# Four stores of a late output piece as operations of their own, and a new order of the last products

## The chip, the core and the metric

The kernel runs on one core of one Trainium2 chip. Times are device microseconds (us) of that core. The profile and its trace come from one profiled execution; "span" is the time from its first to its last recorded instruction. TensorE is called PE, VectorE DVE, ScalarE ACT, GpSimd POOL and SyncE SP, as the profile calls them.

## What is computed

An attention block with polynomial sketch features is followed by a token-mixing block. The attention output of all 4 heads is x, of shape 4 batches x 1088 tokens x 128. Then (reference, cut):

```python
theta = x @ w_theta
zr, zi = x * cos(theta), x * sin(theta)
y = einsum('ts,bsd->btd', w_tok_r, zr) + einsum('ts,bsd->btd', w_tok_i, zi)
u = x + y
out = u + maximum(u @ w_ch, 0)
```

The sum over 1088 source tokens in y is most of the matrix work. `out` is 4 x 1088 x 128 in float32.

## The kernel before

The program is a list of some thousand operations, each with an engine, the buffers that it reads and writes, and a Python function that issues its instructions. Two tables written out by hand decide everything that a scheduler would: `ORDER` is the order in which the operations are issued (each engine works through its own in that order), and `SLOTS` gives each buffer the slot of its class (`big`: 22 slots, one row of token weights each; `g1`, `g3`: output tiles; `ps`: the eight PSUM banks). Waits follow from both: an instruction waits for the producers of its data, and for the last users of its slot.

Batches 0 and 1 go through `mix_row`. Batches 2 and 3 (`PAIR`) are mixed together by `winograd`: seven products of half-size blocks instead of eight, named "1" to "7". Each has 8 or 9 matmuls (one for each 128 source tokens) for each of two column pieces of a half of 544 tokens (`PARTS`: 384 and 160). A finished product is added on DVE to the half that it belongs to, and `done` calls `finish` for both pieces. The text below names the last pieces so:

- **Q384** and **Q160**: batch 3, first half, tokens 0 to 384 and 384 to 544. Their last product is "3".
- **R384** and **R160**: batch 3, second half, last product "7".
- **P384** and **P160**: batch 2, second half, last product "4", the two pieces 384 and 160 tokens wide.

`finish` does for a piece: a matmul with the channel weights (the *output product*, L332), relu and add on DVE (L319), a transpose of 32x32 blocks on DVE into the output tile (L1240), and four stores (L1236), one for each 32 channels. Q384 comes as `ends and t0 == 0`: its four stores are issued inside the transposing operation, one by ACT, one by SP and two by POOL. Q160 takes `finish_turned`: PE transposes the two 80-token halves (L1274), ACT copies them out (L1281), PE makes two output products of 80 tokens (L332, `ps<-w,big`), DVE adds the relu, and SP and ACT store one half each (L1286).

The order of the last operations, from `ORDER` (the width behind each):

- PE: ..., the first matmuls of product 3 for Q160 and R384's output product, product 4 for P384 whole, four matmuls of product 4 for P160 and the last of Q160, the output product of P384, then the last five matmuls of Q384 mixed with the last three of P160; then Q160's transposes, the output product of P160 (160), those of Q160 (80 twice), and the output product of Q384 (384).
- DVE: relu and transposes of batch 2's *first* half stand behind R384's; the last instructions are Q384's addition, P160's relu, Q160's relu, P160's transpose, Q384's relu, Q384's transpose.

At the end of the program SP waits for every DMA in turn, all engines drain and meet in a barrier (L1479).

Of the kernel before, what the change touches and what calls it, by code (L numbers as in the profile page):

```python
# [77 lines left out]
)  # L78
GAPS = {11: 3, 57: 3, 79: 3, 110: 1, 203: 8, 153: 1, 77: 5, 86: 2, 163: 1}
SLOTS = (  # L80
# [11 lines left out]
)  # L92
WARM = 0
LOAD_LEAD = 60.0
# [37 lines left out]
class Layout:  # L132
# [17 lines left out]
    def buf(self, cls, shape, dt, name):  # L150
        b = Buf(cls, shape, dt, name)
        self.bufs.append(b)
        return b
# [92 lines left out]
def kernel(  # L246
# [56 lines left out]
    V, A, G, T, SY = nc.vector, nc.scalar, nc.gpsimd, nc.tensor, nc.sync  # L303
# [14 lines left out]
    def stt(o, a, s, b, op0, op1, eng=None):  # L318
        (eng or V).scalar_tensor_tensor(out=o, in0=a, scalar=s, in1=b, op0=op0, op1=op1)  # L319
# [8 lines left out]
    def vop(n, fn, w, r, due=None, two=False, lk=0):  # L328
        op("V", dve2(n) if two else dve(n), fn, w, r, due, lk=1 if two else lk)

    def mm(o, lhs, rhs, start, stop):
        T.matmul(o, lhs, rhs, start=start, stop=stop, skip_group_check=True)  # L332
# [871 lines left out]
    def mix_out(b, span, yp, due):  # L1204
        g, t0, t1 = span
        xt = xT[b]
        at("out", b, "_", g)
        w = t1 - t0
        xkeys = cells(xt, t0, t1)
        uT = buf("g1", (GW,), F32, "uT")  # L1210
        u = lambda: uT()[:, :w]
        if UDMA[b]:
            op("A", act(w), lambda: A.copy(u(), yp()[:, :w]), [uT], [yp])  # L1213
            join(u, lambda: xt()[:, t0:t1], [uT], xkeys, ADD_FLY2)
        else:
            vop(w, lambda: tt(V, u(), xt()[:, t0:t1], yp()[:, :w], ALU.add), [uT], xkeys + [yp])
        finish(b, t0, w, u, [uT], due)

    def finish(b, t0, w, u, keys, due, ot=None):
        whole = ot is not None  # L1220
        ends = whole and t0 < HT and b == PAIR[1]
        last = not whole or ends or (t0 + w) % HT == 0
        if ends and t0:
            finish_turned(b, t0, w, u, keys, due)
            return
        po = buf("ps", (GW,), F32, "po")
        at0 = t0 % HT if whole else 0
        if not whole:
            ot = buf("g1", (GW,), F32, "ot")
        op("P", w * 4 / 2400 + 0.01, lambda: mm(po()[:, :w], w2()[:, 1], u(), True, True), [po], keys + [w2], hold=[ot])  # L1230
        vop(w, lambda: stt(u(), po()[:, :w], 0.0, u(), ALU.max, ALU.add), keys, [po])
        s0, n = (t0 + w - HT, HT) if whole and not ends else (t0, w)

        def store(E, f0, f1):
            for f in range(f0, f1):
                E.dma_start(out[b, s0:s0 + n, f * SQ:(f + 1) * SQ].rearrange("(c j) i -> j c i", j=SQ),  # L1236
                            ot()[f * SQ:(f + 1) * SQ, :n].rearrange("j (c i) -> j c i", i=SQ))

        def turn():
            V.transpose(out=ot()[:, at0:at0 + w], in_=u())  # L1240
            if ends:
                store(A, 0, 1)
                store(SY, 1, 2)
                store(G, 2, 4)

        vop(w, turn, [(ot, at0)], keys)
        if not last or ends:
            return

        if b == PAIR[0] and t0 >= HT and w == GW:  # L1250
            op("S", w * P * 2 / 100e3, lambda: store(SY, 0, 2), [], [ot], due, lk=2)
            op("A", 0.46, lambda: store(A, 2, 3), [], [ot], due, fly=2.1)
            op("G", 0.9, lambda: store(G, 3, 4), [], [ot], due, fly=2.0)
        elif b == PAIR[0] and t0 >= HT:
            op("A", 0.92, lambda: store(A, 0, 1), [], [ot], due, fly=2.1)
            op("S", w * P * 2 / 100e3, lambda: store(SY, 1, 3), [], [ot], due, lk=1)
            op("G", 0.9, lambda: store(G, 3, 4), [], [ot], due, fly=2.0)
        elif b in PAIR:
            op("S", w * P * 2 / 100e3, lambda: store(SY, 0, 2), [], [ot], due, lk=2)
            op("A", 0.92, lambda: store(A, 2, 4), [], [ot], due, fly=2.1)  # L1260
        elif b and t0 < 2 * GW:
            op("S", w * P * 4 / 100e3, lambda: (store(SY, 0, 2), store(G, 2, 4)), [], [ot], due, lk=4)
        else:
            op("S", w * P * 4 / 100e3, lambda: store(SY, 0, DM // SQ), [], [ot], due, lk=4)

    def finish_turned(b, t0, w, u, keys, due):
        po, pu = (buf("ps", (GW,), F32, x) for x in ("po", "pu"))
        n = w // 2
        yb = buf("g1", (2 * DM,), F32, "yb")
        y = lambda: yb()[:n]  # L1270

        def turned():
            for c in range(2):
                T.transpose(pu()[:n, c * DM:(c + 1) * DM], u()[:, c * n:(c + 1) * n], ident())  # L1274

        def products():
            for c in range(2):
                mm(po()[:n, c * DM:(c + 1) * DM], u()[:, c * n:(c + 1) * n], w2()[:, 1], True, True)

        op("P", 0.2, turned, [pu], keys, hold=[yb])  # L1280
        op("A", act(2 * DM), lambda: A.copy(y(), pu()[:n, 0:2 * DM]), [yb], [pu])  # L1281
        op("P", 0.35, products, [po], keys + [w2])
        vop(2 * DM, lambda: stt(y(), po()[:n, 0:2 * DM], 0.0, y(), ALU.max, ALU.add), [yb], [po])

        def store(E, c):
            E.dma_start(out[b, t0 + c * n:t0 + (c + 1) * n, :], y()[:, c * DM:(c + 1) * DM])  # L1286

        op("S", w * P * 2 / 100e3, lambda: store(SY, 0), [], [yb], due, lk=2)
        op("A", 0.92, lambda: store(A, 1), [], [yb], due, fly=2.1)
# [193 lines left out]
```

## Time and profile before

| what | value |
|---|---|
| runs shown | 218.4 to 219.59 us, median 218.51 us of 3 |
| the profiled execution's own time | 217.77 us |
| its span | 216.0 us, granted TensorE clock 0.997 |
| busy shares of the span | PE 96%, DVE 84%, ACT 53%, POOL 18% |
| in the chain that ended last | PE 58%, DMA 17%, DVE 10%, ACT 9% |

The profiled execution lies 0.74 us below the median; 1.77 us of its time lie outside the span. The chain that ended last is followed back from the last instruction: at each step to what released it. A row of the timeline gives start, length, engine, line, operation and what is written from what, with the number of instructions run together at the end.

### The profile page before, as it was taken

What the parts mean: (1) busy time and instruction counts of PE and PEld (TensorE: products, weight loads), DVE (VectorE), ACT (ScalarE), POOL (GpSimd) and SP (SyncE); (2) the same over time, 40 slices, a digit from 0 to 9 for tenths busy, and PEclk for the clock granted to TensorE, in tenths of its full rate; (3) what the DMA queues carried; (4) which work ended last, traced back from release to release, by engine and by line L of the source; (5) the groups of instructions that cost most, each with busy time, mean ns of one, the idle gap of its engine ahead of it and who ended that gap; (6) DMA issues with size and microseconds to landing.
All of it is one profiled execution on the core that took longest, in us unless ns stands there. A gap on an engine that the chain in (4) does not pass through costs nothing.

```text
span 216.0 us, 5299 instructions
## 1 busy us (share of the span) xinstructions
PE 207.4 (96%) x2140; PEld 150.2 (70%) x2140; DVE 180.7 (84%) x359; ACT 113.5 (53%) x240; POOL 38.5 (18%) x89
## 2 busy tenths in 40 slices
PE   7999999999999999999999999999999999999990
PEld 7777798968767666775656676576766776677660
DVE  1799999999999998998999999979497799955151
ACT  4899999999999896796711423159500000000000
POOL 1182640307300000930003010000220020020013
PEclk9999999999999999999999999999999999999998
DMA  6999999996996994192002244022660012110433
GB/s 226 395 417 418 380 362 420 429 324 143 347 244 230 421 429 177 56 323 49 0 0 36 40 141 113 0 39 108 137 109 0 0 39 50 17 36 4 76 62 67
DMA packets 28044, 37.06 MB, mean 172 GB/s; under 512 B 20564, under 2 KB 23044, under 8 KB 25844
## 3 DMA queue, kind: packets, MB, share of 16 engines
q1 hardware_dynamic: 22868, 31.86, 42.2%
q0 software_dynamic: 1552, 3.25, 7.1%
q10 hardware_dynamic: 3600, 1.62, 2.8%
q8 instruction: 17, 0.28, 0.5%
q14 instruction: 7, 0.06, 0.1%
HBM read 29.84 MB, written 4.00 MB: 157 GB/s over the span
## 4 chain that ended last, share of the span: by engine, by line
PE 58%; DMA 17%; DVE 10%; ACT 9%; issue 3%; SPq 1%; POOL 0%; POOLq 0%; DVEq 0%; ACTq 0%
PE ps L332 54%; DMA zs<-w_tok 11%; DMA zs<-far 2%; DMA st<-s 2%; DVE big L312 2%; ACT big L578 2%; PE ps L951 2%; ACT big L626 2%; DMA far<-zs 1%; DVE g L312 1%; PE ps L1053 1%; DVE big L316 1%; ACT g L726 1%; ACT big L576 1%; PE ps L361 1%
## 5 line engine op out<-in xcount | busy, mean ns | idle before, releaser
L332 PE MATMUL ps<-big,zs 128*128 128x384 f32 (+2 forms) x380 | 108.8, 435 | 0.0
L332 PEld LDWEIGHTS ps<-big,zs 128*128 128x128 f32 x380 | 67.1, 191 | 34.2 <-issue 0.9
L1281 ACT COPY g<-ps 80x256 f32<-80x256 f32 x1 | 0.4, 367 | 54.1 <-PE ps L1274 54.1
L332 PE MATMUL ps<-big,big 128*32 128x32 f32 (+2 forms) x352 | 21.8, 235 | 0.0
L312 DVE CUSTOM_DVE_ANT_0 big<-big,big 128x2176 uint16<-128x2176 uint16 x17 | 21.6, 1281 | 0.1
L578 ACT ACTIVATE big<-zs 128x1088 int32<-128x1088 uint32 (+1 forms) x18 | 21.3, 1190 | 0.7 <-DMA zs<-w_tok 0.7
L576 ACT ACTIVATE big<-zs 128x1088 f32<-128x1088 f32 x17 | 20.9, 1229 | 0.7 <-DMA zs<-w_tok 0.7
L332 PEld LDWEIGHTS ps<-big,big 128*32 128x32 f32 (+1 forms) x352 | 14.9, 125 | 5.6 <-issue 1.0
L312 DVE TENSOR_TENSOR big<-big,big 128x544 f32<-128x544 f32 x24 | 16.7, 713 | 0.1
L326 POOL DMA_DIRECT2D g<-big x6 | 5.3, 1070 | 56.0 <-ACT g L1213 56.0
L1236 POOL DMA_DIRECT2D out<-g x8 | 5.0, 631 | 50.3 <-DVE g L1240 36.0
L312 DVE TENSOR_TENSOR zs<-zs,g 128x384 f32<-128x384 f32 (+2 forms) x24 | 9.9, 449 | 4.0 <-DMA zs<-far 4.0
L316 DVE TENSOR_SCALAR big<-big 128x1088 int32<-128x1088 int32 x17 | 12.3, 721 | 0.0
L361 PE MATMUL ps<-idle 128*128 128x112 bf16 (+1 forms) x67 | 10.0, 312 | 1.3 <-POOL idle L363 1.3
L312 DVE TENSOR_TENSOR g<-lv 128x768 f32<-128x768 f32 x12 | 11.1, 950 | 0.1
L312 DVE TENSOR_TENSOR big<-big,hf 128x1152 f32<-128x1152 f32 x8 | 10.7, 1351 | 0.0
L332 PE MATMUL ps<-mf,big 128*128 128x96 f32 (+1 forms) x72 | 10.0, 278 | 0.4 <-DVE big L312 0.4
L332 PE MATMUL ps<-sbk,g 128*128 128x64 f32 x72 | 10.1, 276 | 0.3 <-ACT g L726 0.3
L332 PE MATMUL ps<-w,big 128*128 128x128 f32 (+1 forms) x76 | 10.2, 278 | 0.0
L332 PEld LDWEIGHTS ps<-w,big 128*128 128x128 f32 (+1 forms) x76 | 9.4, 190 | 0.5
L1139 ACT ACTIVATE g<-g 128x384 f32<-128x384 f32 x12 | 6.3, 532 | 6.7 <-DVE g L319 6.7
L332 PEld LDWEIGHTS ps<-sbk,g 128*128 128x128 f32 x72 | 9.0, 191 | 0.8 <-ACT g L726 0.6
(198 smaller groups left out, 353.0 us busy)
## 6 DMA issues: line engine op xcount, KB each, us to landing
zs<-w_tok SPq DMA_DIRECT2D x17, 1088.0 KB, 10.6
big<-k_l SPq DMA_DIRECT2D x5, 576.0 KB, 12.6
big<-v_l SPq DMA_DIRECT2D x4, 576.0 KB, 15.4
big<-q_l SPq DMA_DIRECT2D x3, 576.0 KB, 10.4
big<-hf POOLq DMA_DIRECT2D x3, 576.0 KB, 9.7
far<-zs SPq DMA_DIRECT2D x3, 576.0 KB, 3.8
zs<-far SPq DMA_DIRECT2D x12, 144.0 KB, 4.1
big<-k_l ACTq DMA_DIRECT2D x2, 576.0 KB, 4.2
```

What stands on the lines that cost most here:

```text
L312: eng.tensor_tensor(out=o, in0=a, in1=b, op=f)
L316: (eng or V).tensor_scalar(out=o, in0=a, scalar1=s1, scalar2=s2, op0=op0, **kw)
L326: op("G", 0.9, lambda: G.dma_start(dst(), src(), accum_op=ALU.add), w, r, fly=fly)
L332: T.matmul(o, lhs, rhs, start=start, stop=stop, skip_group_check=True)
L361: T.matmul(nowhere()[:, :n], idle()[:, 0:P], idle()[:, :n], start=True, stop=True, skip_group_check=True)
L576: op("A", 0.22 + n * 0.0009, lambda: A.activation(dfn(), words_of(raw(), n)[1].bitcast(F32), AF.Prelu, scale=2.0**-112, alpha=-(2.0**32)), ...
L578: op("A", 0.22 + n * 0.0009, lambda: A.activation(stp(), words_of(raw(), n)[0].bitcast(U32), AF.Copy, scale=2.0**-29), [stp], [raw])
L626: op("A", act(n) + 0.1, lambda: A.activation(flat(r()), kc(), AF.Square, accum_out=km()[:, 1:2]), [r, (km, 1)], [kx])
L726: op("A", act(GW), lambda kT=kT, tr=tr: A.copy(kT().rearrange("p c n -> p (c n)"), tr()), [kT], [tr])
L951: T.transpose(tr()[:, i * P:(i + 1) * P], x()[:, g * GC + i].rearrange("p h d -> p (h d)"), ident())
L1139: op("A", act(GW), lambda cs=cs: A.activation(cs()[:, 0], cs()[:, 1], AF.Abs), [(cs, 0)], [(cs, 1)])
L1236: E.dma_start(out[b, s0:s0 + n, f * SQ:(f + 1) * SQ].rearrange("(c j) i -> j c i", j=SQ), ot()[f * SQ:(f + 1) * SQ, :n].rearrange("j (c i) ...
```

## The change

1. Q384's four stores are no longer issued inside the transposing operation. They become two operations behind it: SP issues two, ACT two. POOL issues none of them.
2. `ORDER` is new from the last third of product 7 on. On PE the last five matmuls of Q384 and its output product now stand before product 4; product 4 for P384 and its output product follow, and the three last matmuls of product 3 for Q160 are the last mixing matmuls. Behind them come P160's output product (160), Q160's two transposes and Q160's output products (80 twice). On DVE the relus and transposes of batch 2's first half stand earlier (before R160's), and the last instructions are P160's addition, Q160's addition, P160's relu, P160's transpose and Q160's relu.
3. The stores at the end are in this order: P384 (ACT 1, SP 2, POOL 1), P160 (ACT 1, SP 2, POOL 1), Q160 (SP 1, ACT 1).
4. `SLOTS` is new for some buffers: the rows of token weights 10, 12, 13 and 16, the query features and x of batch 3 change `big` slots among 14, 16, 18, 20 and 21; P160's and Q160's output tiles change places in `g1`; some PSUM banks of the last pieces differ. Up to the last third of product 7 the order of the operations is as before.

No matmul, DVE or ACT operation is added or removed.

```diff
         def turn():
             V.transpose(out=ot()[:, at0:at0 + w], in_=u())
-            if ends:
-                store(A, 0, 1)
-                store(SY, 1, 2)
-                store(G, 2, 4)
 
         vop(w, turn, [(ot, at0)], keys)
-        if not last or ends:
+        if not last:
             return
```

Q384 now falls into the branch that was there for the other pieces of the pair:

```python
        elif b in PAIR:
            op("S", w * P * 2 / 100e3, lambda: store(SY, 0, 2), [], [ot], due, lk=2)
            op("A", 0.92, lambda: store(A, 2, 4), [], [ot], due, fly=2.1)
```

The end of `ORDER` (the last four lines before, the last three after; operation numbers from 919 on are shifted by the two added operations):

```diff
-    912, 979, 980, 958, 959, 823, 826, 827, 969, 913, 970, 971, 972, 973, 974, 975, 976, 977, 981, 982, 983, 824, 623,
-    829, 960, 965, 828, 984, 978, 914, 989, 900, 990, 901, 902, 985, 986, 903, 991, 993, 987, 904, 915, 919, 920, 992,
-    964, 988, 995, 921, 905, 996, 922, 997, 994, 1000, 916, 923, 998, 917, 924, 999, 918,
...
+    949, 901, 950, 902, 960, 903, 904, 964, 971, 965, 908, 961, 962, 905, 981, 916, 982, 917, 983, 972, 973, 974, 975,
+    976, 977, 984, 978, 979, 918, 985, 966, 909, 967, 910, 911, 980, 920, 919, 991, 992, 993, 995, 986, 987, 988, 989,
+    912, 913, 990, 914, 994, 915, 997, 998, 921, 922, 999, 1000, 1001, 923, 924, 925, 926, 996, 1002,
```

Before, 900 to 904 are the last five matmuls of Q384 and 916 its output product; after, both stand in front of product 4 (971 to 979 for P384, 981 to 989 for P160).

22 rows, old and new, of tables (ORDER, SLOTS) are left out of this document.

## Prediction

> **What bounds the kernel now.** I read the page first (shares), then the chain that ended last, then the timeline of the last 25 us, and last the rows of the end of the program (L1479).
>
> ```profile
> PE 207.4 (96%) x2140; PEld 150.2 (70%) x2140; DVE 180.7 (84%) x359; ACT 113.5 (53%) x240; POOL 38.5 (18%) x89
> ```
>
> ```profile
> 117.78 90.94 PE ps L332 x515
> 208.72 0.22 PE ps L1274 x2
> 208.94 0.72 PE ps L332 x6
> ...
> 210.44 0.52 DVE big L319
> 210.95 0.02 issue
> 210.97 0.59 DVE g L1240
> 211.56 0.28 issue
> 211.85 0.64 POOL out L1236
> 212.49 0.60 POOLq L1479
> ```
>
> From 117.78 to 208.72 the chain stands on PE without a break (515 instructions, nothing waited for). The change leaves every matmul in, so until there it can only lose, by making PE wait. What it can win is behind: between the last mixing matmul at 208.72 and the end at 216.0 lie 7.3 us, and they are a chain of their own: DVE's addition, an output product, relu, transpose, two POOL stores one after the other, and the end of the program. These rows of the timeline carry the terms:
>
> ```profile
> 203.87 0.81 PE L332 MATMUL ps<-big,w 128*128 128x384 f32 x2
> 204.52 4.20 PE L332 MATMUL ps<-big,zs 128*128 128x384 f32 x16
> 205.81 0.34 DVE L319 SCALAR_TENSOR_TENSOR big<-ps,even,big 128x160 f32<-128x160 f32 x1
> 208.76 0.62 DVE L319 SCALAR_TENSOR_TENSOR big<-ps,even,big 128x384 f32<-128x384 f32 x1 [0.32 <-PE ps L332]
> 208.98 0.37 ACT L1281 COPY g<-ps 80x256 f32<-80x256 f32 x1 [54.09 <-PE ps L1274]
> 209.05 0.60 PE L332 MATMUL ps<-w,big 128*80 128x128 f32 x4
> 209.30 0.31 DVE L319 SCALAR_TENSOR_TENSOR big<-ps,big 128x160 f32<-128x160 f32 x1
> 209.49 0.86 PE L332 MATMUL ps<-big,w 128*128 128x384 f32 x2
> 209.76 0.42 DVE L319 SCALAR_TENSOR_TENSOR g<-ps,g 80x256 f32<-80x256 f32 x1 [0.15 <-PE ps L332]
> 210.11 0.33 DVE L1240 STREAM_TRANSPOSE g<-big 128x160 f32<-128x160 f32 x1
> 210.65 1.33 SPq L1236 DMA_DIRECT2D out<-g  x3
> 210.73 0.59 POOL L1236 DMA_DIRECT2D out<-g  x1 [3.93 <-DVE g L1240]
> 211.85 1.24 POOL L1236 DMA_DIRECT2D out<-g  x2 [0.52 <-DVE g L1240]
> ```
>
> Behind POOL's last store comes the end of the program; the first three rows are L1479 from 212 on, the others three narrow stretches of the DMA view (issue to landing):
>
> ```profile
> L1479 SPq EVENT_SEMAPHORE  x10: 17/28/87, 212.7 to 214.7; - x10
> L1479 SPq DRAIN  x2: 7/7/7, 214.7 to 214.8; - x2
> L1479 POOLq DRAIN  x1: 2937/2937/2937, 212.3 to 212.3; - x1
> out<-g SPq DMA_DIRECT2D x1, 40.0 KB, 1.5
> out<-g SPq DMA_DIRECT2D x1, 48.0 KB, 2.0
> out<-g POOLq DMA_DIRECT2D x2, 48.0 KB, 2.1
> ```
>
> POOL's two stores end at 211.85 + 1.24 = 213.09, but its drain lasts from 212.29 for 2.94 us, to 215.23, that is 2.14 us after its last store was issued. SP is through its ten waits and its drains at 214.8. So POOL's drain, not SP, lets the barrier go; 216.0 - 215.23 = 0.77 us of barrier follow.
>
> **The change part by part.** *Q384 ahead of product 4.* Its last five matmuls and its output product are only moved. The output product, which stood at the very end (209.49, 0.86 us), now runs where PE is busy anyway, and costs there its pitch: in the row at 203.87 the second of two lasts 0.49 of 0.81, so they start 0.32 apart, 0.65 for both. The last mixing matmul therefore ends at 208.72 + 0.65 = **209.37**, if PE never waits on the way. In return nothing 384 wide is left behind it.
>
> *The new end, Q160.* Addition on DVE: 0.04 to start (208.72 to 208.76), 0.36 long (0.34 in its row), to 209.77. PE's transposes start 0.11 later, as the output product of Q384 did (208.76 + 0.62 = 209.38, start at 209.49): 209.88. This wait is new: before, Q160 was added long before its transposes. P160's output product (160 wide) covers some of it, and about 0.4 us of PE are idle; behind it wait only Q160's own products, and those are in the sum. Transposes 0.22, products 0.60: 210.70. ACT's copy, 0.37, lies beside them. Relu: 0.11 to start (209.65 to 209.76), 0.42 long: 211.23. SP and ACT then issue one store each at about 211.3; with the 1.5 us of the same store before they land at **212.8**.
>
> *P160 beside it.* A 160-wide matmul costs PE 0.27: the row at 204.52 holds five of 384 and three of 160, and 4.20 - 5 x 0.65, less the 0.16 by which the last one ends after its pitch (0.49 - 0.32), leaves 0.8 for the three. P160's output product needs P160's addition (0.34, plus 0.04 and 0.11 around it) while three such matmuls of Q160 run, 0.8 us: no wait. Relu behind Q160's addition, 209.77 + 0.03 + 0.31; transpose 0.03 + 0.33; both to 210.4, as they can overlap a little. POOL's store starts 0.29 after a transpose (210.11 + 0.33 = 210.44 to 210.73) and lasts 0.59: to **211.29**. SP's two stores, at 0.44 each (1.33 for three), are through by 211.3, in front of Q160's store.
>
> *End.* I shift POOL's drain with its last store: 211.29 + 2.14 = 213.43, and 0.77 of barrier: span **214.2** against 216.0, 1.8 us less. SP would be ready some 0.3 to 0.7 us after 212.8 (its ten waits take 0.06 each), so by 213.5 at the latest: about level with POOL.
>
> *The four stores.* Before, Q384 had two POOL stores in a row at the very end (1.24 us, against 0.59 for the one that remains). As SP 2 and ACT 2 they leave around 200 to 201 us, beside PE. A store on SP or ACT also waits for the eighth one before it; those of P160 and Q160 wait for Q384's four and R384's last, and product 4 lies between (9 x 0.65 + 9 x 0.27 = 8.3 us of PE) against 2.0 for a landing. Cost: nothing. If they were late, the last stores would be.
>
> *DVE work moved forward.* Relus and transposes of batch 2's first half now stand earlier, the relus in front of R160's addition. Before, they ran at 196.6 to 199.2 together with R384's:
>
> ```profile
> 189.84 0.57 DVE L1240 STREAM_TRANSPOSE g<-g 128x384 f32<-128x384 f32 x1
> 191.24 0.38 DVE L319 SCALAR_TENSOR_TENSOR big<-ps,even,big 128x160 f32<-128x160 f32 x1 [0.83 <-PE ps L332]
> 191.54 0.55 DVE L312 TENSOR_TENSOR zs<-zs,big 128x384 f32<-128x384 f32 x1
> 192.98 0.43 PE L332 MATMUL ps<-big,w 128*128 128x160 f32 x2
> ...
> 196.64 1.25 DVE L319 SCALAR_TENSOR_TENSOR big<-ps,big 128x384 f32<-128x384 f32 x3 [1.93 <-PE ps L332]
> 197.93 1.26 DVE L1240 STREAM_TRANSPOSE g<-big 128x160 f32<-128x160 f32 x3
> ```
>
> DVE had 0.83 us free before R160's addition (the row at 191.24). In front of it come now the two relus (1.25 less R384's 0.5: about 0.8) and the subtraction of 191.54. DVE, busy until 190.41 before, is through with them at about 191.65. PE's last matmul for R160 comes 0.65 later than before, as one of R384 is put in front of it: 191.24 + 0.65 = 191.89. So PE's end still decides; the sum is ready for PE at 191.89 + 0.38 + 0.11 = 192.4, PE comes to it at 192.98: 0.6 us to spare. Three later places have less: R384's output product 0.35, Q384's 0.25, P384's 0.2 us, each counted as the work that PE has between a product's end and its use, less 0.04 + DVE's instruction + 0.11. So I take 0 for them; if the cover is gone each costs what is missing, 0.2 to 0.3 us, 1 us in all.
>
> *Slots.* The waits that come with them are for things long done, but one: ACT's squares of the queries of batch 3 (L924) now wait for DVE's sum over a weight row.
>
> ```profile
> 66.09 2.49 DVE L312 CUSTOM_DVE_ANT_0 big<-big,big 128x2176 uint16<-128x2176 uint16 x2
> 68.45 1.16 ACT L924 ACTIVATE big<-big 128x1152 f32<-128x1152 f32 x1
> ```
>
> It is the first of the two, over at about 67.35; ACT comes at 68.45. Cost 0, with 1.1 us to spare.
>
> The Trainium skill, "VectorE: DVE Perf Modes", section "The DRAIN you can't avoid", says that the drains at a program's start and end are boilerplate of about 12 ns on all five engines. SP's 7 ns agree; POOL's 2937 ns do not, so here the row decides. By the page POOL would hold nothing, and SP's waits would set the end: rival 1.
>
> **The rivals.**
>
> 1. *POOL's drain does not follow its last store.* For it: a drain that was fetched at 212.29, before the last store started (213.09 - 0.6 = 212.49), may have its length from something else. Then SP ends it: landing 212.8, up to 0.5 for its waits, 0.77: span 214.05, gain 1.95.
> 2. *The last stores of SP and ACT land like those of 48 KB, in 2.0 us.* They go out with P160's beside them. Landing 213.3, SP through at 213.9, span 214.7, gain 1.3.
> 3. *PE waits for DVE on the way.* All four narrow places are missed by 0.2 to 0.3 us: the last mixing matmul comes 1 us later, gain 0.8. Against it: through the same sequence of products, with as many instructions of DVE between them, PE's row in the chain has no break.
> 4. *Slower: the new wait of ACT at 68.45.* Were DVE over 1.1 us later there than in this profile, each further us would hold ACT, and with it the features of batch 3 that PE needs in turn. To make the kernel slower by more than 0.5% it must eat the gain and 1.1 us more: DVE 4 us late, about 219.8 us. Against it: nothing before that place is moved, so DVE has no reason to be late.
>
> That the change does not do what it says is part of the sum: POOL still issues two stores in the last 3 us, only one of them last.
>
> **How the numbers follow.** The sum is made against the profiled execution, 217.77 us, and gives 215.97. That execution lies 0.74 below the median of the runs shown, 218.51; a median of the changed kernel is foretold from it: 218.51 - 1.8 = **216.7**. Chances: forecast 0.56 (216.7), rival 1 0.12 (216.55), rival 2 0.12 (217.2), rival 3 0.14 (217.7), rival 4 0.06 (219.8). Half a per cent, 1.1 us, is about what a measurement of this kernel can tell from no change; the bound is 217.4. Faster are the first three: 0.80; the same is rival 3: 0.14; slower rival 4: 0.06. The range takes in the forecast and rivals 1 and 2, with the spread of the runs around them (the fastest 0.1 under the median, the profiled one 0.74 under it): 216.0 to 217.6.
>
> **What would show it.** Right: in the chain of the changed kernel PE stands without a break to about 209.4, then Q160's addition (0.36), L1274, `ps<-w,big`, the 80x256 relu at about 210.8; POOL's last store at 210.7, its drain ending near 213.4. Rival 1: that drain short, SP's waits last. Rival 2: landing of the L1286 stores 2.0. Rival 3: DVE named as releaser of PE between 192 and 209. Rival 4: PE's long stretch starting later than 117.8. I am wrong if the last mixing matmul ends after 210, or if the interval from POOL's last store to the end is not 2.9 us.

## The result, and the profile after

| | before | after |
|---|---|---|
| median of the runs | 218.4 us (7 runs, 217.34 to 219.59) | 216.51 us (7 runs, 215.9 to 217.45) |
| ratio, with its 95% interval | | 0.9924 (0.9896 to 0.9952) |
| profiled execution, its span | 217.77, 216.0 us | 215.9, 214.1 us |
| PE's unbroken stretch to the last mixing matmul | 117.78 to 208.72 (90.94) | 117.62 to 209.20 (91.58) |
| from there to the end of the span (the *tail*) | 7.28 us | 4.9 us |

The kernel became faster by 0.76%, 1.9 us (1.0 to 2.3 by the interval), against 216.7 us and a gain of 1.8 foretold. The last two rows of the table are the whole change in two numbers, for the two profiled executions, which both lie 0.6 us under their medians: the mixing is 0.64 longer, the tail 2.4 shorter, and the stretch began 0.16 earlier.

Of the page of the changed kernel, the busy times:

```profile
PE 207.0 (97%) x2140; PEld 149.7 (70%) x2140; DVE 180.7 (84%) x359; ACT 113.4 (53%) x240; POOL 37.2 (17%) x87
```

Instructions of PE, DVE and ACT are as many as before; POOL has two fewer, the two stores of Q384. Busy times do not show the gain. The timeline does; a row is start, length, engine, line, operation, written from read, count, and in brackets the idle time in front and what ended it:

```profile
206.50 0.81 PE L332 MATMUL ps<-big,w 128*128 128x384 f32 x2
...
207.14 2.06 PE L332 MATMUL ps<-big,zs 128*128 128x160 f32 x14
...
209.04 0.43 PE L332 MATMUL ps<-big,w 128*128 128x160 f32 x2
209.25 0.38 DVE L319 SCALAR_TENSOR_TENSOR big<-ps,even,big 128x160 f32<-128x160 f32 x1 [0.50 <-PE ps L332]
...
209.68 0.41 PE L1270 MATMUL ps<-ident,big 128*80 128x128 f32 x2 [0.21 <-DVE big L319]
...
209.94 0.60 PE L332 MATMUL ps<-w,big 128*80 128x128 f32 x4
...
210.53 0.59 POOL L1236 DMA_DIRECT2D out<-g  x1 [1.11 <-DVE g L1240]
...
210.63 0.42 DVE L319 SCALAR_TENSOR_TENSOR g<-ps,g 80x256 f32<-80x256 f32 x1 [0.39 <-DMA out<-g]
...
211.08 0.37 ACTq L1282 DMA_DIRECT2D out<-g  x1
211.16 0.38 SPq L1282 DMA_DIRECT2D out<-g  x1
```

The last mixing matmul ends at 207.14 + 2.06 = 209.20. Behind it nothing of the chain is 384 wide: for Q160 a 160-wide addition (0.38), two transposes, two 80-token products, a relu of 0.42 and two stores, and beside it P160's output product, relu, transpose and stores. The products are over 1.34 us after the last mixing matmul (209.94 + 0.60 = 210.54); before, the last product ended at 210.35, 1.63 after it, and DVE still had 384-wide work. POOL's only store here is P160's; before, two 48 KB stores ran from 211.85 to 213.09.

The end of the program (rows of L1475; count, then shortest, median and longest in ns, then the first and last start), first all from 205 us on, then a window from 212.7 to 213.5:

```profile
L1475 POOLq DRAIN  x3: 34/93/2502, 210.5 to 213.9; - x3
L1475 SPq EVENT_SEMAPHORE  x11: 17/28/28, 211.6 to 214.1; - x11
L1475 SPq DRAIN  x3: 7/7/13, 213.3 to 213.6; - x3
```

```profile
L1475 SPq EVENT_SEMAPHORE  x8: 27/28/28, 212.8 to 213.2; - x8
L1475 SPq DRAIN  x2: 7/10/13, 213.3 to 213.4; - x2
```

POOL's long drain starts at 210.51 and is over at 213.01. SP's last drain of the first round is at 213.4. So SP, not POOL, now lets the barrier go, by some 0.4 us: eight of its waits follow one another in 212.8 to 213.2, 0.06 apart. The first of them ends when SP's own last store lands (211.16 + 1.6 = 212.8), and none of the others is held by anything any more. SP was held by one early wait, and then walked the rest of the list.

The chain that ended last is a trap here. Its last rows in the changed kernel:

```profile
190.23 0.61 POOL out L1236
190.85 17.95 issue
208.81 0.61 POOL out L1236
209.42 1.09 issue
210.51 0.62 POOLq L1475
```

The view walks back from POOL's last instruction through POOL's drain and its stores, and leaves PE aside from 171 us on. The row "issue" of 17.95 us gives it away: for that time the view found nothing that POOL waited for, so these steps bound nothing. In the profile before, the same view happened to go along PE to the end. That PE stands without a break to the last mixing matmul, a sign that the prediction wanted to read from this chain, has to be read from PE's waits instead (shown further down).

### The profile page after: what moved, and what is told of

It reads as the page before. It is cut to its first block, busy times and chain, and to the rows that moved or that the text cites. A ratio compares the mean times of both kernels' runs of the same rounds, so it can differ in the third digit from the quotient of the medians.

```text
span 214.1 us, 5301 instructions
## 1 busy us (share of the span) xinstructions
PE 207.0 (97%) x2140; PEld 149.7 (70%) x2140; DVE 180.7 (84%) x359; ACT 113.4 (53%) x240; POOL 37.2 (17%) x87
## 4 chain that ended last, share of the span: by engine, by line
PE 55%; DVE 18%; issue 11%; ACT 6%; DMA 6%; POOL 1%; SPq 1%; POOLq 0%; DVEq 0%; ACTq 0%
PE ps L332 49%; DVE big L312 7%; DMA zs<-far 3%; DMA st<-s 2%; PE ps L1053 2%; PE ps L951 2%; ACT big L626 2%; DVE big L319 1%; DMA far<-zs 1%; DVE g L312 1%; DVE zs L312 1%; DVE big L316 1%; ACT g L726 1%; PE ps L361 1%; POOL out L1236 1%
## 5 line engine op out<-in xcount | busy, mean ns | idle before, releaser
L1236 POOL DMA_DIRECT2D out<-g x6 | 3.8, 633 | 49.7 <-DVE g L1240 31.8
```

## The experiments

All stand beside runs of the kernel before on the same chip, with medians of 218.33 us beside e1 to e4 and 218.4 us beside the others. For each, two numbers are read from its profile: the *mixing* (from the first `ps<-mf,big` matmul of PE's stretch to the end of the last mixing matmul; 90.94 before, 91.58 after) and the *tail*. The theory was: the order of the last products carries the gain, through the width of what is left behind the last mixing matmul, and the stores are worth something only where they stand at the end. The rival: the stores alone carry it, as POOL's two stores and its drain are what ended last. A further one: the gain is given back on the way by PE waiting for DVE.

| kernel | median us (ratio, 95% interval) | stretch starts | mixing | tail |
|---|---|---|---|---|
| e1_stores_only | 217.69 (0.9976, 0.9957 to 0.9996) | 118.36 | 90.94 | 6.80 |
| e2_old_stores | 216.62 (0.9926, 0.9901 to 0.9952) | 119.04 | 91.58 | 4.68 |
| e3_q384_last | 217.97 (0.9987, 0.9968 to 1.0007) | 117.80 | 90.95 | 6.95 |
| e4_slots_only | 218.25 (0.9997, 0.9964 to 1.003) | 117.88 | 90.94 | 7.28 |
| e5_dve_late | 216.83, one run | 118.12 | 92.00 | 4.98 |
| e6_lane | 218.31, one run | 120.29 | 91.57 | 4.64 |
| e7_no_pool | 216.13 (0.9916, 0.9886 to 0.9946) | 119.29 | 91.58 | 4.73 |
| after_again | 216.93 (0.9934, 0.991 to 0.9958) | 118.99 | 91.58 | 4.93 |

The spans have one decimal, so a tail is good to 0.05. The mixing repeats to 0.01 us in kernels of the same order, and the tail to 0.1 where all stores are the same too (4.9, 4.93 and 4.98; 7.28 twice). Each pair of mixing and tail comes from one profiled execution. What scatters from execution to execution is the start of the stretch, 117.6 to 120.3, so the steps are judged by mixing and tail.

**The stores alone, in the order of before** (e1_stores_only):

```diff
             if ends:
-                store(A, 0, 1)
-                store(SY, 1, 2)
-                store(G, 2, 4)
+                store(SY, 0, 2)
+                store(A, 2, 4)
```

> The order of before; only Q384's four stores are changed, two on SP and two on ACT, none on POOL. My theory (the order of the last products carries most of the gain, the stores less): the transpose of Q384 still ends at about 211.6; SP's and ACT's second stores start at about 212.0, land 2.0 later at 214.0 to 214.1, SP's walk over its waits takes up to 0.6 and the barrier 0.75: span 214.9 to 215.4, against 216.0 before and 214.1 for the change. Rival (POOL's two stores at the end are all of it): span 214.1, the whole gain.

The median is 0.24% under before's, and the tail 0.48 shorter. The span, 216.1, lies above what was expected; with the stretch starting 0.58 later than before's (118.36 against 117.78) it would be 215.5, still 0.1 off. Its timeline and the end of its program show why POOL gone is worth no more than that:

```profile
211.23 1.91 SPq L1236 DMA_DIRECT2D out<-g  x4
211.31 0.60 POOL L1236 DMA_DIRECT2D out<-g  x1 [3.93 <-DVE g L1240]
...
211.41 0.47 ACTq L1285 DMA_DIRECT2D out<-g  x1
...
212.17 0.91 ACTq L1236 DMA_DIRECT2D out<-g  x2
```

```profile
L1478 POOLq DRAIN  x3: 34/93/2578, 211.3 to 215.9; - x3
L1478 SPq DRAIN  x3: 7/7/13, 215.3 to 215.6; - x3
```

POOL is drained at 213.9, 1.5 us before SP (215.4). SP issues four stores in a row from 211.23 to 213.14, the last two of them Q384's, which DVE transposes last. A wait took the place of the one removed: SP's own queue and its last landing. So the rival, that the stores alone carry the gain, gets between a quarter and a third of it: 0.48 of the 1.74 us by which mixing and tail together became shorter, or 0.24% of 0.76%.

**The new order, with the stores of before** (e2_old_stores): Q384's four stores are back inside the transposing operation (ACT 1, SP 1, POOL 2), and its two new operations issue nothing.

> The changed kernel with Q384's four stores as before (ACT 1, SP 1, POOL 2, issued inside the transposing operation). My theory: in the new order they leave at about 201 us, beside PE, and POOL has 7 us free behind them: span 214.1 as in the changed kernel, within 0.2. Rival (the stores are the gain): span back toward 216.0.

The median is 0.9926 of before, the same as the change's 0.9924, and the tail, 4.68, is if anything shorter. Q384's POOL stores stand far from the end:

```profile
202.52 1.22 POOL L1236 DMA_DIRECT2D out<-g  x2 [10.25 <-DVE g L1240]
...
210.23 0.61 POOL L1236 DMA_DIRECT2D out<-g  x1 [6.48 <-DVE big L312]
```

In the new order the stores of point 1 are worth nothing. They and the order do not add up. In this kernel POOL's drain is last again: it starts at 211.9 and takes 2.59, to 214.5, SP's last drain is at 214.4.

**The changed kernel, with Q384's last part at the end again** (e3_q384_last): its output product, relu, transpose and stores stand behind those of Q160, the new stores stay.

```diff
-    949, 901, 950, 902, 960, 903, 904, 964, 971, 965, 908, 961, 962, 905, 981, 916, 982, 917, 983, 972, 973, 974, 975,
-    976, 977, 984, 978, 979, 918, 985, 966, 909, 967, 910, 911, 980, 920, 919, 991, 992, 993, 995, 986, 987, 988, 989,
-    912, 913, 990, 914, 994, 915, 997, 998, 921, 922, 999, 1000, 1001, 923, 924, 925, 926, 996, 1002,
+    949, 901, 950, 902, 960, 903, 904, 964, 971, 965, 908, 961, 962, 905, 981, 982, 983, 972, 973, 974, 975,
+    976, 977, 984, 978, 979, 985, 966, 909, 967, 910, 911, 980, 991, 992, 993, 995, 986, 987, 988, 989,
+    912, 913, 990, 914, 994, 915, 997, 998, 921, 922, 999, 1000, 1001, 923, 924, 925, 926, 916, 917, 918, 920, 919, 996, 1002,
```

> The changed kernel, its new stores kept, but Q384's output product, relu, transpose and stores are put behind Q160's (operations 916 to 920 behind 926). My theory: the last mixing matmul ends 0.65 earlier, at 208.56; Q384's output product runs 209.7 to 210.6, relu to 211.2, transpose to 211.8, second stores of SP and ACT start at 212.2 and land at 214.2; with SP's walk and the barrier the span is 215.1 to 215.6, 1.0 to 1.5 over the changed kernel. Rival (the stores are the gain): span 214.1.

Nearly all of the gain is gone: ratio 0.9987, an interval that takes in 1. The mixing is back at 90.95, as the output product no longer stands among it, and the tail at 6.95. The span is 215.7, and 215.5 without the 0.18 by which its stretch starts later than the change's. Its last matmuls and stores:

```profile
209.47 0.60 PE L332 MATMUL ps<-w,big 128*80 128x128 f32 x4
...
209.91 0.81 PE L332 MATMUL ps<-big,w 128*128 128x384 f32 x2
...
211.95 0.85 SPq L1236 DMA_DIRECT2D out<-g  x2
211.96 0.91 ACTq L1236 DMA_DIRECT2D out<-g  x2
```

The 384-wide product ends at 210.72, and only 1.2 us later, behind relu and transpose, do its stores go out. This is the cost of a wide piece at the end: not the product (0.65) but what follows it in turn. Width is not tried apart from form here: Q384 is transposed on DVE and leaves in four stores, Q160 is turned on PE and leaves in two. The rows price the width in each link (relu 0.56 against 0.31, transpose 0.58 against 0.34), but no run puts a narrow piece of Q384's form at the end.

**Only the slots** (e4_slots_only): the kernel before with the new slots of class `big`.

> The kernel before with the new slots of the class big alone (weight rows 10, 12, 13, 16, the query features and x of batch 3); order, stores and the other slots as before. My theory: 0, a span of 216.0 within 0.2, PE's unbroken stretch starting at 117.6 to 117.8. Rival (the slots carry part of the gain, or cost some): the stretch starts elsewhere by over 0.3, and the span moves with it.

Mixing 90.94, tail 7.28, ratio 0.9997: nothing that the interval of 0.3% to both sides would show. The stretch starts at 117.88, a little later than expected. The new slots of output tiles and PSUM banks belong to the new order and were not tried apart from it.

**Two of the narrow places, made late** (e5_dve_late): the changed kernel, with an additional DVE instruction in front of R160's last addition (160 wide) and of P384's addition (384 wide); its result goes to a buffer that nobody reads.

> The changed kernel with two more DVE instructions that lead nowhere: in front of R160's last addition one 160 wide (0.32 us), in front of P384's addition one 384 wide (0.55 us), each reading the same bank as the addition behind it. My theory (the places have the margins of the sum, 0.6 and 0.2 us, and beyond them PE loses one for one): R160's output product is not late; P384's addition comes 0.46 later, PE waits 0.25 in front of P384's output product, named as waiting for DVE L312, and the stretch from the last mixing matmul to the end stays 4.9. Rival (the margins are not what decides, PE runs on elsewhere): no wait of PE on DVE there; or both cost the full 0.3 and 0.5.

At R160, with some 0.35 us added, PE comes through unmoved; at P384, with 0.6 added, PE waits. The timeline around P384:

```profile
203.71 3.46 PE L332 MATMUL ps<-big,zs 128*128 128x384 f32 x16
...
206.11 0.56 DVE L312 TENSOR_TENSOR junk<-big,ps 128x384 f32<-128x384 f32 x1 [4.80 <-PE ps L332]
206.70 0.55 DVE L312 TENSOR_TENSOR big<-big,ps 128x384 f32<-128x384 f32 x1
...
207.31 0.91 PE L332 MATMUL ps<-big,w 128*128 128x384 f32 x2
...
208.06 2.06 PE L332 MATMUL ps<-big,zs 128*128 128x160 f32 x14
```

The mixing is 92.00, 0.42 longer: 0.3 to the start of the output product (207.31, where 206.50 and the 0.50 by which this stretch starts later give 207.00), and 0.1 more as its two matmuls no longer follow close upon others (0.91 instead of 0.81). That is more than the 0.25 expected, as DVE's addition comes 0.6 later and not 0.46. And the view of waits does not name DVE here, which was expected too: the matmul before the product ends at 207.16, so that the records leave only 0.15 us idle. So the spare time at P384 is real and small, about 0.2 us, and what is missed beyond it (0.6 - 0.2) goes into the end one to one. This is one execution, and the place at R160 was not pushed beyond its 0.6.

**Where SP's walk ends** (e6_lane, e7_no_pool). Two kernels move the stores of the end. e6_lane stores P384 by SP 1, ACT 1 and POOL 2 instead of SP 2, ACT 1, POOL 1:

```diff
-            op("S", w * P * 2 / 100e3, lambda: store(SY, 0, 2), [], [ot], due, lk=2)
-            op("A", 0.46, lambda: store(A, 2, 3), [], [ot], due, fly=2.1)
-            op("G", 0.9, lambda: store(G, 3, 4), [], [ot], due, fly=2.0)
+            op("S", w * P * 2 / 100e3, lambda: store(SY, 0, 1), [], [ot], due, lk=2)
+            op("A", 0.46, lambda: store(A, 1, 2), [], [ot], due, fly=2.1)
+            op("G", 0.9, lambda: store(G, 2, 4), [], [ot], due, fly=2.0)
```

> The changed kernel with one store of P384 given from SP to POOL, so that P384 has SP 1, ACT 1, POOL 2. The last two stores then have completion semaphores that SP asks for last, not second. Theory of the end (SP asks for the semaphores one after the other, 0.06 us each, also for those long done, so what lands last should be asked last): from the last landing to SP's last drain some 0.2 us instead of 0.6; then POOL's drain, about 2 us behind its last store, ends last: 4.6 to 4.7 us from the last mixing matmul to the end, against 4.9. Rival (the walk costs nothing, it lies beside POOL's drain): 4.9.

Tail 4.64, 0.25 to 0.3 under the change's, and as expected POOL's drain is now last: it starts at 213.18 and takes 2.55, to 215.72; SP's last drain starts at 215.65. The time of this one run, 218.31, says nothing of that: its stretch starts 2.7 us later, for a reason some 18 us further up (last section).

e7_no_pool takes POOL out of P160, so that POOL's last store is P384's at 210.48, and gives Q384's last two stores to POOL (they stand at 202.77):

```diff
-            op("A", 0.92, lambda: store(A, 0, 1), [], [ot], due, fly=2.1)
-            op("S", w * P * 2 / 100e3, lambda: store(SY, 1, 3), [], [ot], due, lk=1)
-            op("G", 0.9, lambda: store(G, 3, 4), [], [ot], due, fly=2.0)
+            op("A", 0.92, lambda: store(A, 0, 2), [], [ot], due, fly=2.1)
+            op("S", w * P * 2 / 100e3, lambda: store(SY, 2, 4), [], [ot], due, lk=1)
+            op("G", 0.9, lambda: None, [], [ot], due, fly=2.0)
+        elif ends:
+            op("S", w * P * 2 / 100e3, lambda: (store(SY, 0, 1), store(G, 2, 4)), [], [ot], due, lk=2)
+            op("A", 0.92, lambda: store(A, 1, 2), [], [ot], due, fly=2.1)
```

> The changed kernel, P160 stored by SP 2 and ACT 2 and Q384 by SP 1, ACT 1 and POOL 2: POOL's last store is P384's, 2 us earlier, and the stores that land last have the semaphore asked for last. Theory of the end: POOL's drain ends at least 1 us before SP, SP's last drain comes 0.2 us behind the last landing: 4.4 to 4.5 us from the last mixing matmul to the end, against 4.9 for the change, 0.2% of the time. Rival (POOL's drain has its length from something else, or a fourth store on ACT delays Q160's): 4.7 or more.

Tail 4.73: 0.2 shorter, about half of what was expected. The last stores, and the end from 210 to 215 us:

```profile
211.95 0.86 ACTq L1236 DMA_DIRECT2D out<-g  x2
...
212.83 0.38 SPq L1285 DMA_DIRECT2D out<-g  x1
212.91 0.39 ACTq L1285 DMA_DIRECT2D out<-g  x1
```

```profile
L1478 POOLq DRAIN  x1: 2982/2982/2982, 210.5 to 210.5; - x1
L1478 SPq EVENT_SEMAPHORE  x10: 17/28/28, 213.3 to 215.0; - x10
L1478 SPq DRAIN  x2: 7/7/7, 214.8 to 214.8; - x2
```

POOL is drained at 213.4, more than a microsecond before SP, and the tail hardly notices: with the change as it is, POOL no longer holds the end. The 0.2 can come from SP's list alone, which is nearly at its end when the last store lands. Part of that is lost again at ACT's last store, which now leaves behind SP's instead of ahead of it (212.91; it is ACT's third in a row). Its 216.13 us are the lowest median of all, but its interval overlaps that of the changed kernel (0.9934 beside it), so it is faster than the kernel before, and not shown to be faster than the change.

**The changed kernel once more** (after_again), as a measure for the others.

> The changed kernel once more, on the same chip as the run without POOL's late store: 4.9 us from the last mixing matmul to the end, ratio to before 0.990 to 0.995. What varies is the start of PE's unbroken stretch, 117.6 to 119 us in the runs so far.

Mixing 91.58 and tail 4.93 repeat; the span, 215.5 against 214.1, differs by the 1.37 us by which the stretch starts later.

## Why the prediction was right, point by point

- **Q384's output product costs the mixing its pitch, 0.65.** Measured 0.64 (90.94 to 91.58), in four kernels of that order; e3_q384_last, which takes it out, is back at 90.95.
- **PE does not wait on the way.** All four narrow places came out as counted. The rows of the changed kernel, DVE's addition and the product that needs it (R160, R384, Q384; P384's product is the row at 206.50 above):

```profile
191.73 0.39 DVE L319 SCALAR_TENSOR_TENSOR big<-ps,even,big 128x160 f32<-128x160 f32 x1 [0.34 <-PE ps L332]
...
192.81 0.43 PE L332 MATMUL ps<-big,w 128*128 128x160 f32 x2
...
194.58 0.62 DVE L319 SCALAR_TENSOR_TENSOR big<-ps,even,big 128x384 f32<-128x384 f32 x1 [1.76 <-PE ps L332]
...
195.67 0.81 PE L332 MATMUL ps<-big,w 128*128 128x384 f32 x2
...
197.80 0.62 DVE L319 SCALAR_TENSOR_TENSOR big<-ps,even,big 128x384 f32<-128x384 f32 x1
...
198.79 0.81 PE L332 MATMUL ps<-big,w 128*128 128x384 f32 x2
...
205.61 0.56 DVE L312 TENSOR_TENSOR big<-big,ps 128x384 f32<-128x384 f32 x1 [4.80 <-PE ps L332]
```

  (The rows of other engines between them are left out.) From the end of the addition, less the 0.11 to PE, to the product: 192.81 - 192.12 - 0.11 = 0.58 at R160 (0.6 foretold), 0.36 at R384 (0.35), 0.26 at Q384 (0.25), and 206.50 - 206.17 - 0.11 = 0.22 at P384 (0.2). At Q384 the output product does not stand wholly in front of product 4, as the section on the change has it: in `ORDER` the first matmul of product 4 for each piece (971, 981) stands between Q384's last matmul (904) and its output product (916), and these two are part of the work that covers DVE's addition. The view of waits has for PE from 60 us on only these three in the changed kernel:

```profile
PE ps L332 <- DVE big L312: 0.4, 1, 0.4
PE ps L332 <- DVE zs L312: 0.3, 1, 0.3
PE ps L1270 <- DVE big L319: 0.2, 1, 0.2
```

  The first stands at 117.6, the second at 100.5, the third is Q160's and was in the sum. Rival 3 did not come. e5_dve_late shows that it could have: with 0.6 us more of DVE in front of P384's addition, PE comes 0.4 us late to the end of the mixing.
- **The new end.** Products over at 210.54 (210.70 foretold), relu at 211.05 (211.23), P160's POOL store 210.53 to 211.12 (210.70 to 211.29), the last stores at 211.08 and 211.16 (about 211.3), landing in 1.5 and 1.6 (1.5). Each is 0.15 to 0.2 early, and 0.16 of that is the start of PE's stretch, which no step spoke of. Rival 2 did not come: stores of 40 KB land in 1.5 to 1.6 beside others, too.
- **Q384's new stores cost nothing, and bring nothing by themselves.** The first was said. The second was not worked out: the text counts them as a part of a new end. e2_old_stores shows that in the new order it does not matter who issues them; e1_stores_only, that in the old order they give 0.5 us of tail. In the new order the tail is even 0.2 shorter without them (4.68 against 4.9): with two stores fewer on SP and ACT, the last stores have other semaphores, and SP has fewer left to ask for (last section).
- **What holds the end: here the step was off, and the sum not.** The prediction shifted POOL's drain with its store (2.14 behind it, to 213.43) and put SP level with it, at 213.5 at the latest. Measured: POOL's drain ends 1.89 behind its store, at 213.01, and SP, at 213.4, is last. The drain follows the landing of the store, and P160's 20 KB landed in 1.8 us where Q384's 48 KB had taken 2.1; that is why a shift by 2.14 was too much. So rival 1 had the right place and the wrong cause: SP, not the drain, ends the program, but the drain still follows its store, and SP ends at the upper end of the time that both texts gave it. That the interval from POOL's last store to the end is still 2.98 us (2.9 foretold) is a coincidence. The Trainium skill, "VectorE: DVE Perf Modes", section "The DRAIN you can't avoid", has such drains at about 12 ns; the measurements decide otherwise for POOL, whose first drain took 2499 to 2982 ns in all ten profiles here, and agree for SP (7 to 13 ns).
- **Slots and the wait at L924.** e4_slots_only: nothing. ACT's squares start at 68.53 in the changed kernel, 68.45 before. Rival 4 had no part: where the stretch of other profiles starts later than 117.8, its sign, that comes from a wait near 100 us (last section).

What the prediction gives as 1.8 us came as 1.9 in the profiled pair: -2.4 of tail, +0.64 of mixing, -0.16 of scatter in the start. Its sign of being wrong, a last mixing matmul that ends after 210, was no safe one: it ends at 209.20 here, but at 210.57 in after_again, where the stretch starts later and mixing and tail are the same.

## What to carry to other kernels

Order the last pieces so that a narrow one is last: what stands behind the last matmul of the long stretch is a chain of addition, product, relu, transpose and store, and each link costs more for a wide piece, while the wide piece's product costs only its pitch when it stands inside the stretch. A store at the very end is judged by the whole list that follows it (the queue of its engine, its landing, the walk of SP over the semaphores, POOL's drain); moving it helps only until the next of these is late, which is why the gains of the stores and of the order did not add up here. And where executions scatter, compare stretches between fixed instructions, not spans.

## What the runs showed of the hardware

- **POOL's drain follows the landing of its last store, not its issue.** It ended about 0.7 us after that landing in all profiles: in the changed kernel the store of 210.53 landed in 1.8, the drain was over at 213.01; in e7_no_pool the store of 210.48 landed in 2.25, at 212.7, the drain was over at 213.4. That is a regularity of these profiles; the drain alone was not measured.
- **SP asks for the semaphores in a fixed order, 0.06 us each.** What counts is not which store lands last, but landing plus the rest of the list. In the changed kernel SP had eight waits from the landing that held it on (212.8 to 213.2), in e2_old_stores two (a window from 214.2 to 214.6):

```profile
L1482 SPq EVENT_SEMAPHORE  x2: 28/28/28, 214.2 to 214.3; - x2
L1482 POOLq DRAIN  x1: 2589/2589/2589, 211.9 to 211.9; - x1
```

  The tail of that kernel is 0.2 shorter, with the same stores at the end. Six waits of 0.06 less are nearly 0.4; the gain stops at 0.2, because POOL's drain (211.9 + 2.59 = 214.5) then ends last. That the order of the list is the cause was read from the traces, and not tried by itself.
- **The scatter of nearly 3 us between executions arises near 100 us**, where PE waits for DVE's products of x (`zs<-zs,g`). For this x is written to memory and read back in another order (`far<-zs`, then four reads `zs<-far`). The row of the changed kernel, from a view up to 104 us, and that of e6_lane:

```profile
100.46 3.71 PE L332 MATMUL ps<-big,zs 128*128 128x320 f32 x11 [0.27 <-DVE zs L312]
```

```profile
102.02 5.72 PE L332 MATMUL ps<-big,zs 128*128 128x320 f32 x12 [1.86 <-DVE zs L312]
```

  In both the last of the four reads is issued at 94.2. It lands 5.4 us later in the first, where DVE waits 1.16 us for it, and 7.0 us later in e6_lane. In the ten profiles PE's wait here goes from under 0.15 us to 1.86, and the later starts of the stretch stand beside the longer waits. Why the read comes late in one execution and not in another stays open; at 1.6 us it is nearly as large as the whole change.
- **Behind the longest of these waits the granted clock was lower.** In e6_lane it was 0.50 from 102.4 to 105.7 us, where the changed kernel had 1.00: twelve matmuls took 5.72 us there, eleven 3.71 in the changed kernel. Half the clock for some 3.4 us costs about 1.7 us; with the 1.6 us of waiting this accounts for e6_lane's 2.7, as PE then no longer waits 0.4 us at the start of the stretch. Behind the wait of 1.48 us in e7_no_pool the clock stayed at 1.00. One profile does not show that the wait brought the lower clock about.
